# The second layer's products in a new order: 18 up, 15 down, 3 up, 9 down

## The chip, the core and the metric

The kernel runs on one core of a Trainium2 chip. A core has five engines that run side by side, each through its own queue of instructions in the order of the program, and that wait for one another by semaphores: TensorE (matrix products, from SBUF into the banks of PSUM), VectorE and ScalarE (element-wise work, from and to SBUF and PSUM), GpSimd and SyncE (here mostly DMA issue). The metric is the time of one execution on the device in microseconds, as the median of several runs.

## What is computed

```python
X = np.fft.rfft(x, axis=1); Y = X * F; y = np.fft.irfft(Y, n=S, axis=1)   # x: 8 x 3072 x 256
# a mixture of eight experts with one expert per token, 256 -> 1024 -> 256
h = np.maximum(x[mask] @ w1[e], 0.0); out[mask] = gate_w * eom * (h @ w2[e])
# the second layer, on all 24576 tokens, 256 -> 2048 -> 256
h = np.maximum(x @ w_in, 0.0)
return (h * h @ w_out).astype(np.float32)
```

The change is in the last two lines, the second layer.

## The kernel before

The program runs through a spectral stage (two transforms and a filter), a routing and first expert layer, and then the second layer, which is what matters here. It works in tiles of 512 tokens, 48 of them (`NTILE2`), and each tile in eight units (`NU`), each of 256 of the 2048 hidden columns. So `units2` holds 384 units, and the loop at the end of `steps_m` walks over them.

All products are made to nearly single precision from two halves: every operand has a high part and a low part, and one product is three matmuls into the same PSUM bank (high by high, high by low, low by high), each 128 x 128 by 128 x 256.

A unit has an up part and a down part. Up (`up2`) multiplies a 2 x 2 arrangement of blocks (tokens by columns) by seven products in place of eight, Strassen's way in Winograd's form. The sums of weight blocks (`wsh`, `wsl`) and of input blocks (`bh`, `bl`) are made ahead of time. The seven products go into three banks: V gets products 0, 4, 5 and 2 one on top of the other, G gets 3 and 6, P gets 1. Between two products on one bank the partial sum must be read out: ScalarE copies V after product 0 into `s1`, G after product 3 into `p5`, V after product 4 into `u2`, V at the end into `C[:, 2]`. VectorE adds P and `s1` into `C[:, 0]`, V and `p5` into `C[:, 3]`, G and `u2` into `C[:, 1]`. A product that goes onto a bank with a partial sum waits until that sum has been read. V has two banks that alternate from unit to unit (`psH`), G and P have one each (`psX`, `psH2`). In the trace the tile of V and P is called ph, that of G px, and `s1`, `p5`, `u2` are s, p, u.

Then VectorE makes the squared rectified hidden values in one instruction, `q = max(C, 0) * C` (L923), ScalarE casts them to the high part `hh` (L930), and VectorE subtracts to get the low part `hl` (L932); the last two are in `split_h`. Down (`down2`) multiplies `hh` and `hl` by `woh` and `wol`: 24 matmuls (L945) that are summed over the eight units of a tile in two banks (py). In the last unit of a tile each bank is copied out by ScalarE after matmul 11 and 23 (L951) and scattered to the output by DMAs of GpSimd (L954).

All three are Python generators. The order in which the loop resumes them is the order in which each engine gets its instructions; nothing reorders them later. In iteration n the loop interleaves up of unit n, the split of unit n-1 and down of unit n-2, in four parts. Before the change TensorE gets products 0, 3 (six matmuls), down's 0 to 2, products 1, 4, down's 3 to 8, products 6, 5, down's 9 to 17, product 2, down's 18 to 23. One iteration is 21 matmuls of up and 24 of down.

Beside it, the inputs of the next tile are loaded (`load_t`, in unit 2) and split (`split_t`, L865 to L889, one step at the end of each of units 3 to 6).

Of the kernel before, what the change touches and what calls it, by code (L numbers as in the profile page):

```python
# [17 lines left out]
ALU = mybir.AluOpType  # L18
# [84 lines left out]
def spectral_moe_kernel(ctx: ExitStack, tc: tile.TileContext, x, filt_r, filt_i, w_gate, w_og, w1, w2,  # L103
                        w_in, w_out, c_ma, c_mi, c_mb, c_mb2, c_sg, c_cum, out):
    nc = tc.nc
# [608 lines left out]
    def py_tiles(t):  # L714
        return [pl["psY2" if t % 2 and "psY2" in pl else "psY"].tile([128, TT], F32, name=f"py{h}") for h in range(2)]
# [82 lines left out]
    def up(t, f):  # L798
        xh, xl = X[t]
        w = width[t]  # L800
        h1, l1 = (a[:, 0] for a in W[t, f // 2])
        f2 = f % 2
        ps = ph_tile()[:, 0:w]
        n = 0
        for c in range(2):
            for a, b in ((h1, xh), (h1, xl), (l1, xh)):
                nc.tensor.matmul(ps, a[:, c, f2 * 128:(f2 + 1) * 128], b[:, c, 0:w], start=n == 0, stop=n == 5)  # L807
                n += 1
        hh = pl["hp"].tile([128, TT], F32R, name="hh")[:, 0:w]
        hl = pl["hp"].tile([128, TT], F32R, name="hl")[:, 0:w]  # L810
        nc.scalar.activation(hh, ps, AF.Relu)  # L811
        tick[:] = [hh[0:1, 0:1].bitcast(F32)]
        nc.vector.scalar_tensor_tensor(hl, ps, 0.0, hh.bitcast(F32), op0=ALU.max, op1=ALU.subtract)  # L813
        H[t, f] = hh, hl
# [77 lines left out]
    def up2(t, u):  # L892

        bh, bl, _ = X2[t]
        wsh, wsl = w2nd[0:2]

        def prod(ps, a, b, start):
            for n, (x, y) in enumerate(((wsh, bh), (wsh, bl), (wsl, bh))):
                nc.tensor.matmul(ps, x[:, u, a], y[:, b], start=start and n == 0, stop=n == 2, skip_group_check=True)  # L899

        bank = lambda name: pl[name].tile([128, TT], F32, name="px" if name == "psX" else "ph")[:, 0:256]
        V, G, P = bank("psH"), bank("psX"), bank("psH2")
        s1, p5, u2 = (pl["sp"].tile([128, 256], F32, name=n) for n in ("s1", "p5", "u2"))
        C = pl["cp"].tile([128, 4, 256], F32, name="C")
        prod(V, 0, 0, True)
        nc.scalar.copy(s1, V)
        prod(G, 3, 3, True)
        nc.scalar.copy(p5, G)
        yield
        prod(P, 1, 1, True)  # L910
        nc.vector.tensor_tensor(C[:, 0], P, s1, ALU.add)
        prod(V, 4, 4, False)
        nc.scalar.copy(u2, V)
        yield
        prod(G, 6, 2, False)
        prod(V, 5, 5, False)
        nc.vector.tensor_tensor(C[:, 3], V, p5, ALU.add)  # L917
        nc.vector.tensor_tensor(C[:, 1], G, u2, ALU.add)
        yield
        prod(V, 2, 6, False)  # L920
        nc.scalar.copy(C[:, 2], V)  # L921
        q = pl["cp"].tile([128, 4, 256], F32, name="q")
        nc.vector.scalar_tensor_tensor(q, C, 0.0, C, op0=ALU.max, op1=ALU.mult)  # L923
        H2[t, u] = q
        yield

    def split_h(t, u):
        q = H2[t, u]
        hh, hl = (pl["h2p"].tile([128, 4, 256], F32R, name=n) for n in ("hh2", "hl2"))
        nc.scalar.copy(hh, q)  # L930
        yield
        nc.vector.tensor_tensor(hl, q, hh.bitcast(F32), ALU.subtract)  # L932
        H2[t, u] = hh, hl
        yield

    def down2(t, u):

        hh, hl = H2[t, u]
        woh, wol = w2nd[2:4]
        if u == 0:  # L940
            Z[t] = [p.rearrange("p (c d) -> p c d", c=2) for p in py_tiles(t)]
        for m in range(24):
            k, i, c, n = m // 12, m // 6 % 2, m // 3 % 2, m % 3
            x, w = ((hh, woh), (hl, woh), (hh, wol))[n]
            nc.tensor.matmul(Z[t][k][:, c, :], x[:, 2 * i + k, c * 128:(c + 1) * 128], w[:, 2 * u + i, :],  # L945
                             start=u == 0 and m in (0, 12), stop=u == NU - 1 and m in (11, 23), skip_group_check=True)
            if u == NU - 1 and m in (11, 23):
                if k == 0:
                    Z[t].append(pl["oup"].tile([128, 4, D], F32, name="ou"))
                ou = Z[t][2]  # L950
                nc.scalar.copy(ou[:, 2 * k:2 * k + 2, :], Z[t][k])  # L951
                io = X2[t][2]
                for c in range(2 * k, 2 * k + 2):
                    nc.gpsimd.indirect_dma_start(out=outv[4 * t + c], out_offset=bass.IndirectOffsetOnAxis(ap=io[:, c:c + 1], axis=0),  # L954
                                                 in_=ou[:, c, :], in_offset=None)
            if m in (2, 8, 17):
                yield
        del H2[t, u]
        if u == NU - 1:
            del X2[t], Z[t]  # L960
        yield
# [3 lines left out]
    units2 = [(t, u) for t in range(NTILE2) for u in range(NU)]  # L965
# [3 lines left out]
    def step_1(t, f):  # L969

        last = t + 1 == KP
        if f == 5 and t + 2 == KP:
            start_t(KP)
        if f == 1 and t + 1 >= KP:
            for n in (t + 2, t + 3) if last else (t + 3,):
                if n < NMAIN:
                    start_t(n)
        if f == 1 and last:
            gather(KP)
        if f == 3 and t + 2 < NMAIN and t + 2 != KP:  # L980
            gather(t + 2)
        if f % 2 == 1:

            g = NQ * t + f // 2 + 2
            if NQ * KP <= g < NQ * NMAIN:
                split_w(*divmod(g, NQ))
            if NQ * KP <= g + 2 < NQ * NMAIN:
                load_w(*divmod(g + 2, NQ))
        if t + 1 < NMAIN:
            at = (4, 5, 7) if last else (2, 4, 6)  # L990
            if f == at[0]:
                scale_x(t + 1)
            if f == at[0] + 1:
                put_ids(t + 1)
            if f in at[1:]:
                turn_x(t + 1, at.index(f) - 1)
        elif f == 1:
            load_t(0)
            load_t(1)
        if f not in (1, 5) and dec and next(dec[0], 0) == 0:  # L1000
            dec.clear()
            dcs.close()
            pl["bp0"] = ctx.enter_context(tc.tile_pool(name="bp0", bufs=1))
            pl["bp0"].tile([128, 16], F32, name="pad0")
        if t + 1 == NMAIN and f >= 3:
            if f == 3:
                first.append(split_t(0))
            next(first[0], None)

    def extra(t):  # L1010

        start_t(t)
        gather(t)
        for q in range(3):
            load_w(t, q)
        scale_x(t)
        put_ids(t)
        turn_x(t, 0)
        turn_x(t, 1)
        for f in range(NF + 1):  # L1020
            if f < NF:
                if f % 2 == 0:
                    split_w(t, f // 2)
                    if f == 0:
                        load_w(t, 3)
                up(t, f)
            if f:
                down(t, f - 1)

    def rest(t):  # L1030

        if t < NTILE1:
            with tc.If(used[0] > slot[t - KP]):
                extra(t)
                rest(t + 1)
# [3 lines left out]
    def steps_m():  # L1039
        for n in range(len(jobs) + LAG1):  # L1040
            if n < len(jobs):
                t, f = jobs[n]
                up(t, f)
                step_1(t, f)
            if n >= LAG1:
                down(*jobs[n - LAG1])
            yield
        used.append(nc.values_load(usedi[0:1, 0:1], min_val=0, max_val=NTILE_T))
        with tc.If(used[0] > NTILE_T - NX):
            extra(NMAIN)  # L1050
            rest(NMAIN + 1)
        m1.close()
        xgs.close()
        open_m2()
        st = iter(())
        for n in range(len(units2) + 2):
            g = up2(*units2[n]) if n < len(units2) else iter(())
            t, u = units2[min(n, len(units2) - 1)]
            d = down2(*units2[n - 2]) if n >= 2 else iter(())
            for part in range(4):  # L1060
                next(g, None)
                if part == 0 and 0 < n <= len(units2):
                    sh = split_h(*units2[n - 1])
                if part in (1, 2) and n:
                    next(sh, None)
                next(d, None)
            if u == 2 and t + 2 < NTILE2:
                load_t(t + 2)
            if u == 3 and t + 1 < NTILE2:
                st = split_t(t + 1)  # L1070
            next(st, None)
            yield
# [43 lines left out]
    m = steps_m()  # L1116
# [4 lines left out]
    for i, k in enumerate(order):  # L1121
# [3 lines left out]
        n = done["a"]  # L1125
# [62 lines left out]
```

## Time and profile before

| what | us |
|---|---|
| median of 3 runs | 3807.01 (3805.06 to 3810.75) |
| the profiled execution, whole | 3809.94 |
| its span, from first to last instruction | 3808.2 |
| the second layer's matmuls, first to last | 1777.4 to 3797 |

The profile is of one execution. A page sums it up; the rest are answers to questions put to its trace. In the views below a line of the timeline is one instruction: its start from the start of the span, its duration, its engine (PE is TensorE's matmuls, PEld its loads of stationary weights, DVE is VectorE, ACT ScalarE), its line in the program, what it writes and reads, and, in brackets, how long the engine stood idle ahead of it and what it waited for. Matmuls are pipelined, so a matmul's duration is much longer than the distance from its start to the next one's start; the distance is what counts.

### The profile page before, as it was taken

What the parts mean: (1) busy time and instruction counts of PE and PEld (TensorE: products, weight loads), DVE (VectorE), ACT (ScalarE), POOL (GpSimd) and SP (SyncE); (2) the same over time, 40 slices, a digit from 0 to 9 for tenths busy, and PEclk for the clock granted to TensorE, in tenths of its full rate; (3) what the DMA queues carried; (4) which work ended last, traced back from release to release, by engine and by line L of the source; (5) the groups of instructions that cost most, each with busy time, mean ns of one, the idle gap of its engine ahead of it and who ended that gap; (6) DMA issues with size and microseconds to landing.
All of it is one profiled execution on the core that took longest, in us unless ns stands there. A gap on an engine that the chain in (4) does not pass through costs nothing.

```text
span 3808.2 us, 73021 instructions
## 1 busy us (share of the span) xinstructions
PE 3750.1 (98%) x27156; PEld 3501.1 (92%) x27156; DVE 2759.2 (72%) x5024; ACT 1966.4 (52%) x3896; POOL 607.0 (16%) x641
## 2 busy tenths in 40 slices
PE   8999999999999999999999999999999999999998
PEld 7888877888888888888999999999999999999998
DVE  6677685678878875656777777777777777777775
ACT  6466473354545454554555555555555555555554
POOL 3477574000000000000011001000100110011001
PEclk9999999999999999999999999999999999999999
DMA  6333322455555554543000100010000001000100
GB/s 193 101 114 116 105 81 95 149 161 165 174 159 176 165 165 154 158 159 95 24 26 27 29 23 29 23 29 23 29 24 28 24 29 29 23 26 26 29 18 18
DMA packets 259756, 306.63 MB, mean 81 GB/s; under 512 B 74721, under 2 KB 203202, under 8 KB 259394
## 3 DMA queue, kind: packets, MB, share of 16 engines
q1 hardware_dynamic: 239936, 249.75, 21.6%
q0 software_dynamic: 18432, 51.93, 3.8%
q8 instruction: 214, 3.51, 0.4%
q14 instruction: 148, 1.21, 0.1%
q10 hardware_dynamic: 1026, 0.23, 0.0%
HBM read 221.63 MB, written 80.19 MB: 79 GB/s over the span
## 4 chain that ended last, share of the span: by engine, by line
PE 84%; issue 10%; DVE 2%; POOL 1%; DMA 1%; ACT 1%; another core or an unknown queue 0%; DVEq 0%; POOLq 0%; ACTq 0%; SPq 0%
PE py L945 22%; PE ph L899 14%; PE ph L807 14%; PE py L824 14%; PE px L899 6%; PE o L360 3%; PE p L380 3%; PE o L394 2%; PE p L281 2%; PE p L334 1%; PE p L338 1%; PE p L309 1%; POOL out_dram L954 1%; PE px L787 1%; DMA xt<-in_x_dram 0%
## 5 line engine op out<-in xcount | busy, mean ns | idle before, releaser
L945 PE MATMUL py<-woh,hh 128*128 128x256 f32 x3072 | 857.2, 279 | 0.0
L945 PE MATMUL py<-woh,hl 128*128 128x256 f32 x3072 | 852.8, 278 | 0.4 <-DVE hl L932 0.4
L945 PE MATMUL py<-wol,hh 128*128 128x256 f32 x3072 | 852.9, 278 | 0.0
L954 POOL DMA_INDIRECT out_dram<-ou,ix x192 | 213.2, 1110 | 2912.9 <-ACT ou L951 2869.0
L945 PEld LDWEIGHTS py<-woh,hl 128*128 128x128 f32 x3072 | 579.9, 189 | 0.9 <-DVE hl L932 0.8
L945 PEld LDWEIGHTS py<-woh,hh 128*128 128x128 f32 x3072 | 579.9, 189 | 0.0
L945 PEld LDWEIGHTS py<-wol,hh 128*128 128x128 f32 x3072 | 576.3, 188 | 0.0
L899 PE MATMUL ph<-bh,wsh 128*128 128x256 f32 x1920 | 540.9, 282 | 5.9 <-DMA ytd<-yt 4.6
L811 ACT ACTIVATE hh<-ph 128x512 fp32r<-128x512 f32 (+1 forms) x464 | 248.7, 536 | 574.8 <-PE ph L807 548.8
L899 PE MATMUL ph<-bl,wsh 128*128 128x256 f32 x1920 | 537.1, 280 | 0.0
L899 PE MATMUL ph<-bh,wsl 128*128 128x256 f32 x1920 | 536.7, 280 | 0.0
L923 DVE SCALAR_TENSOR_TENSOR q<-C 128x1024 f32<-128x1024 f32 x384 | 470.5, 1225 | 6.4 <-ACT C L921 6.4
L932 DVE TENSOR_TENSOR hl<-q,hh 128x1024 fp32r<-128x1024 f32 x384 | 467.1, 1216 | 1.1 <-ACT hh L930 1.1
L813 DVE SCALAR_TENSOR_TENSOR hl<-ph,hh 128x512 fp32r<-128x512 f32 (+1 forms) x464 | 283.3, 611 | 252.0 <-ACT hh L811 244.2
L917 DVE TENSOR_TENSOR C<-ph,p 128x256 f32<-128x256 f32 x384 | 163.6, 426 | 412.8 <-ACT hh L930 402.5
L921 ACT COPY C<-ph 128x256 f32<-128x256 f32 x384 | 143.4, 373 | 532.4 <-PE ph L899 500.2
L930 ACT CAST hh<-q 128x1024 fp32r<-128x1024 f32 x384 | 402.8, 1049 | 1.3 <-DVE q L923 1.3
L899 PEld LDWEIGHTS ph<-bh,wsh 128*128 128x128 f32 x1920 | 362.3, 189 | 7.1 <-issue 4.7
L899 PEld LDWEIGHTS ph<-bl,wsh 128*128 128x128 f32 x1920 | 360.9, 188 | 0.0
L899 PEld LDWEIGHTS ph<-bh,wsl 128*128 128x128 f32 x1920 | 360.8, 188 | 0.0
L824 PE MATMUL py<-hh,wh 128*128 128x512 f32 (+1 forms) x928 | 336.6, 369 | 0.0
L807 PE MATMUL ph<-xh,wh 128*128 128x512 f32 (+1 forms) x928 | 335.2, 361 | 0.0
(265 smaller groups left out, 8045.4 us busy)
## 6 DMA issues: line engine op xcount, KB each, us to landing
r<-in_moe_w_dram SPq DMA_DIRECT2D x440, 256.0 KB
xt<-in_x_dram SPq DMA_DIRECT2D x48, 512.0 KB
r<-ytd SPq DMA_DIRECT2D x48, 512.0 KB
xg<-srt SPq DMA_DIRECT2D x41, 544.0 KB
ytd<-yt SPq DMA_DIRECT2D x41, 512.0 KB
xg<-srt SPq DMA_DIRECT2D x17, 272.0 KB
ytd<-yt SPq DMA_DIRECT2D x17, 256.0 KB
raw<-in_moe_w_in_dram SPq DMA_DIRECT2D x16, 256.0 KB
```

Of the source, the lines that this page charges most:

```text
L807: nc.tensor.matmul(ps, a[:, c, f2 * 128:(f2 + 1) * 128], b[:, c, 0:w], start=n == 0, stop=n == 5)
L811: nc.scalar.activation(hh, ps, AF.Relu)
L813: nc.vector.scalar_tensor_tensor(hl, ps, 0.0, hh.bitcast(F32), op0=ALU.max, op1=ALU.subtract)
L824: nc.tensor.matmul(Y[t][h], a[:, f % 2, h * 128:(h + 1) * 128], b, start=f == 0 and i == 0, stop=f == NF - 1 and i == 2, skip_group_check= ...
L899: nc.tensor.matmul(ps, x[:, u, a], y[:, b], start=start and n == 0, stop=n == 2, skip_group_check=True)
L917: nc.vector.tensor_tensor(C[:, 3], V, p5, ALU.add)
L921: nc.scalar.copy(C[:, 2], V)
L923: nc.vector.scalar_tensor_tensor(q, C, 0.0, C, op0=ALU.max, op1=ALU.mult)
L930: nc.scalar.copy(hh, q)
L932: nc.vector.tensor_tensor(hl, q, hh.bitcast(F32), ALU.subtract)
L945: nc.tensor.matmul(Z[t][k][:, c, :], x[:, 2 * i + k, c * 128:(c + 1) * 128], w[:, 2 * u + i, :], start=u == 0 and m in (0, 12), stop=u == ...
L954: nc.gpsimd.indirect_dma_start(out=outv[4 * t + c], out_offset=bass.IndirectOffsetOnAxis(ap=io[:, c:c + 1], axis=0), in_=ou[:, c, :], in_o ...
```

## The change

It moves the points at which `up2` and `down2` give control back, and the loop's calls. Up of a unit now reaches into the next iteration: the loop keeps the generator of the unit before in `old` and resumes it three times, once for product 2 (behind product 0 of the new unit), once for ScalarE's copy into `C[:, 2]` (behind the copy into `p5`), once for VectorE's square (behind the sum into `C[:, 0]`). TensorE's order in iteration n becomes: product 0 of unit n, product 2 of unit n-1, products 3, 1, 4, 6 of unit n, down's 0 to 14 of unit n-2, product 5 of unit n, down's 15 to 23. ScalarE's order: `s1`, `p5`, `C[:, 2]` of unit n-1, `u2`, `hh` of unit n-1. VectorE's: `C[:, 0]`, the square of unit n-1, `C[:, 1]`, `C[:, 3]`, `hl` of unit n-1.

```diff
         prod(V, 0, 0, True)
         nc.scalar.copy(s1, V)
+        yield
         prod(G, 3, 3, True)
         nc.scalar.copy(p5, G)
         yield
         prod(P, 1, 1, True)
         nc.vector.tensor_tensor(C[:, 0], P, s1, ALU.add)
+        yield
         prod(V, 4, 4, False)
         nc.scalar.copy(u2, V)
-        yield
         prod(G, 6, 2, False)
+        nc.vector.tensor_tensor(C[:, 1], G, u2, ALU.add)
+        yield
         prod(V, 5, 5, False)
         nc.vector.tensor_tensor(C[:, 3], V, p5, ALU.add)
-        nc.vector.tensor_tensor(C[:, 1], G, u2, ALU.add)
         yield
         prod(V, 2, 6, False)
+        yield
         nc.scalar.copy(C[:, 2], V)
+        yield
         q = pl["cp"].tile([128, 4, 256], F32, name="q")
         nc.vector.scalar_tensor_tensor(q, C, 0.0, C, op0=ALU.max, op1=ALU.mult)
         H2[t, u] = q
...
-            if m in (2, 8, 17):
+            if m in (5, 14):
                 yield
...
         st = iter(())
+        none = iter(())
+        old = none
         for n in range(len(units2) + 2):
-            g = up2(*units2[n]) if n < len(units2) else iter(())
+            g = up2(*units2[n]) if n < len(units2) else none
             t, u = units2[min(n, len(units2) - 1)]
-            d = down2(*units2[n - 2]) if n >= 2 else iter(())
-            for part in range(4):
-                next(g, None)
-                if part == 0 and 0 < n <= len(units2):
-                    sh = split_h(*units2[n - 1])
-                if part in (1, 2) and n:
-                    next(sh, None)
-                next(d, None)
+            d = down2(*units2[n - 2]) if n >= 2 else none
+            next(g, None)
+            next(old, None)
+            next(g, None)
+            next(old, None)
+            next(g, None)
+            next(old, None)
+            sh = split_h(*units2[n - 1]) if 0 < n <= len(units2) else none
+            next(g, None)
+            next(sh, None)
+            next(d, None)
+            next(d, None)
+            next(g, None)
+            next(sh, None)
+            next(d, None)
+            old = g
             if u == 2 and t + 2 < NTILE2:
```

## Rows read from the trace of the kernel before

**Rows 1.** The page: the span, and each engine's busy time.

```profile
span 3808.2 us, 73021 instructions
PE 3750.1 (98%) x27156; PEld 3501.1 (92%) x27156; DVE 2759.2 (72%) x5024; ACT 1966.4 (52%) x3896; POOL 607.0 (16%) x641
```

**Rows 2.** Table by stretch: length, busy time per engine, granted clock, DMA share, GB/s.

```profile
1800.00:3790.00 1990.00, 1990.00 (x17065) 1989.74 (x17064) 1464.93 (x2270) 1033.33 (x2175) 209.35 (x188) 1.00 0.09 26
```

**Rows 3.** Timeline, TensorE: one unit's blocks by first matmul, and twenty units on.

```profile
2605.18 0.28 PE L899 MATMUL ph<-bh,wsh 128*128 128x256 f32 x1
...
2606.25 0.28 PE L899 MATMUL ph<-bh,wsh 128*128 128x256 f32 x1
...
2606.60 0.28 PE L899 MATMUL ph<-bh,wsh 128*128 128x256 f32 x1
...
2607.62 0.28 PE L899 MATMUL px<-bh,wsh 128*128 128x256 f32 x1
...
2608.34 0.28 PE L945 MATMUL py<-woh,hh 128*128 128x256 f32 x1
...
2609.40 0.28 PE L899 MATMUL ph<-bh,wsh 128*128 128x256 f32 x1
...
2610.43 0.28 PE L899 MATMUL ph<-bh,wsh 128*128 128x256 f32 x1
...
2710.14 0.28 PE L899 MATMUL ph<-bh,wsh 128*128 128x256 f32 x1
```

**Rows 4.** Timeline: a weight load, a product's last matmul, and copies of idle ScalarE.

```profile
2606.49 0.28 PE L899 MATMUL ph<-bh,wsl 128*128 128x256 f32 x1
2606.49 0.19 PEld L899 LDWEIGHTS ph<-bh,wsh 128*128 128x128 f32 x1
...
2606.83 0.28 PE L899 MATMUL ph<-bh,wsl 128*128 128x256 f32 x1
...
2607.20 0.37 ACT L913 COPY u<-ph 128x256 f32<-128x256 f32 x1 [0.57 <-PE ph L899]
...
2611.04 0.37 ACT L906 COPY s<-ph 128x256 f32<-128x256 f32 x1 [0.66 <-PE ph L899]
```

**Rows 5.** Timeline, the layer's first units: loads that wait, and matmuls behind them.

```profile
1782.90 0.37 ACT L906 COPY s<-ph 128x256 f32<-128x256 f32 x1
...
1783.32 0.19 PEld L899 LDWEIGHTS ph<-bh,wsh 128*128 128x128 f32 x1
...
1783.54 0.28 PE L899 MATMUL ph<-bl,wsh 128*128 128x256 f32 x1
...
1784.02 0.28 PE L899 MATMUL px<-bh,wsl 128*128 128x256 f32 x1
...
1785.61 0.19 PEld L899 LDWEIGHTS ph<-bh,wsh 128*128 128x128 f32 x1 [0.79 <-DVE C L917]
...
1785.83 0.28 PE L899 MATMUL ph<-bl,wsh 128*128 128x256 f32 x1
...
1786.07 0.28 PE L899 MATMUL ph<-bh,wsh 128*128 128x256 f32 x1
...
1786.41 0.28 PE L899 MATMUL px<-bh,wsh 128*128 128x256 f32 x1
```

**Rows 6.** Groups of instructions, 1800 to 3790 us: busy us, mean ns, idle before.

```profile
L930 ACT CAST hh<-q 128x1024 fp32r<-128x1024 f32 x380 | 398.6, 1049 | 0.0
...
L923 DVE SCALAR_TENSOR_TENSOR q<-C 128x1024 f32<-128x1024 f32 x379 | 464.4, 1225 | 5.6 <-ACT C L921 5.6
L932 DVE TENSOR_TENSOR hl<-q,hh 128x1024 fp32r<-128x1024 f32 x379 | 461.0, 1216 | 0.0
...
L885 DVE TENSOR_TENSOR tc<-r,tc 128x256 f32<-128x256 f32 x94 | 39.6, 421 | 1.6
```

**Rows 7.** Timeline, the layer's end: the last product 2, and the last load that waits.

```profile
3790.15 0.28 PE L899 MATMUL ph<-bh,wsh 128*128 128x256 f32 x1
...
3794.78 0.19 PEld L945 LDWEIGHTS py<-woh,hl 128*128 128x128 f32 x1 [0.59 <-DVE hl L932]
```

More of the change, by code (lines that the diff above doesn't have):

```diff
@@ L911, in up2 @@
         nc.vector.tensor_tensor(C[:, 0], P, s1, ALU.add)
+        yield
         prod(V, 4, 4, False)
         nc.scalar.copy(u2, V)
+        prod(G, 6, 2, False)
+        nc.vector.tensor_tensor(C[:, 1], G, u2, ALU.add)
         yield
-        prod(G, 6, 2, False)
         prod(V, 5, 5, False)
         nc.vector.tensor_tensor(C[:, 3], V, p5, ALU.add)
-        nc.vector.tensor_tensor(C[:, 1], G, u2, ALU.add)
         yield
         prod(V, 2, 6, False)
+        yield
         nc.scalar.copy(C[:, 2], V)
+        yield
         q = pl["cp"].tile([128, 4, 256], F32, name="q")
```

## Prediction

> **What bounds the kernel now.** I read the page first: its span is 3808.2 us and TensorE is busy for 98% of it [rows 1]. A busy TensorE need not be one at its peak, so the second view is the table by stretch: from 1800 to 3790 us, which is the second layer, TensorE has 1990.00 us of work in 1990.00 us, 17065 matmuls, with a granted clock of 1.00, the 2.4 GHz level [rows 2]. That is 0.1166 us for each matmul, 5.248 us for a unit of 45. The timeline says the same: twenty units from 2605.18 to 2710.14 take 104.96 us [rows 3]. VectorE is busy for 1464.93 us of the stretch and ScalarE for 1033.33, so both have room, and nothing but the matmuls' own spacing, or a new wait of TensorE, moves the end.
>
> The third view is one unit by its matmuls [rows 3]. The reader should see that the spacing is not one number. Nine matmuls from 2606.60 to 2607.62 come every 0.1133 us; nine from 2608.34 to 2609.40 every 0.1178 us. I call these paces quick and slow. The clock is the same in both. The pace changes where a stretch of down products gives way to up products: at 2605.18 to slow, at 2606.25 to quick, at 2607.62 to slow, at 2609.40 to quick, at 2610.43 to slow again, four changes in a unit. Where up gives way to down (2608.34, for one) the pace is kept. All quick, a unit would be 45 x 0.1133 = 5.10 us. The first slow block costs 2606.25 - 2605.18 - 9 x 0.1133 = 0.05 us, the second 2609.40 - 2607.62 - 15 x 0.1133 = 0.08, and each quick block 0.01 to get going (1.37 against 12 x 0.1133, 1.03 against 9 x 0.1133). Together 0.15, which is the 5.248 measured.
>
> **The change: what stays.** Per unit there are the same 45 matmuls and the same ten instructions of ScalarE and VectorE. No DMA is added; the two output copies and four output DMAs of a tile's last unit keep their places behind down's matmuls 11 and 23. What changes is the order. Call the products by their operand's place: V0, G3, P1, V4, G6, V5, V2. The loop now gives TensorE V0, V2 of the unit before, G3, P1, V4, G6 (18 matmuls), fifteen of down, V5 (three), nine of down. ScalarE gets s1, p5, the copy of C[:,2] of the unit before, u2, the cast hh; VectorE gets C[:,0], the square, C[:,1], C[:,3], then hl.
>
> **The change: the new wait.** G6 adds onto the bank that G3 filled, and p5 must have read that bank first. Before, fifteen matmuls lay between the two. Now only P1 and V4 do, six matmuls. The way from G3's last matmul to the load of G6's weights goes by three rows. From the start of a product's last matmul to the start of an idle ScalarE's copy: 2607.20 - 2606.83 = 0.37 us [rows 4]. The copy: 0.37 us [rows 4]. From a copy's end to the load that it lets go: s1 ended at 1782.90 + 0.37 = 1783.27, the load came at 1783.32, so 0.05 [rows 5]. Sum 0.79 us. ScalarE is idle when G3 ends: s1 starts 2611.04 - 2610.43 = 0.61 us into a unit [rows 3, 4] and takes 0.37, while p5 can start only 8 x 0.1133 + 0.37 = 1.28 us into it. The load is due when the matmul before it starts, as at 2606.49 in [rows 4], so 6 x 0.1133 = 0.68 us after G3's last: it is 0.11 us late in every unit. After such a wait nothing is caught up: a held load went at 1785.61, the second matmul behind it at 1785.83, twice a quick step, and two more took 0.24 us to 1786.07 [rows 5], against 0.227 quick, so 0.01 more. Price: 0.12 us per unit. Bounds: nothing, if the wait held the matmul and not its load (below), and 0.13, with the rows' roundings against it.
>
> The Trainium skill, "TensorE: Matmul & The Clock Gate", section "Architectural detail: the array is 16× 32×32, not 1× 128×128", says that TensorE's queue can pull weight loads ahead of matmuls in flight. By that rule the load would not be late, and the wait would cost nothing. The trace does not bear it out for a load that has to wait: the load at 1785.61 stands behind the wait for C [rows 5].
>
> **The change: the pace.** Two changes from down to up are left of four, at V0 and at V5. The trace before has no block of 18 or 15, so the pace of each is bounded by the two that it has. I take it that the pace still turns over at each such change. Which half is slow then hangs on the pace after the new wait. Rows for that lie far apart: after the full stop at 1785.61 the three matmuls from 1786.07 to 1786.41 were quick, while after the load that was only 0.05 us late at 1783.32 four matmuls took 1784.02 - 1783.54 = 0.48 us, slow [rows 5]. At 0.11 us the load starts when its matmul was due, as in a full stop, so I take quick. G6 and fifteen of down are then quick, V5 and nine of down slow, and V0 turns to quick again. A slow block of twelve lies between the block of nine (0.05) and that of fifteen (0.08): 0.065, and 0.01 to get going. Unit: 5.10 + 0.12 + 0.075 = 5.295 us, 0.047 more than 5.248; times 384 units, +18 us.
>
> **The change: other waits.** V4 waits for s1, nine matmuls after V0, as before. V5 waits for u2, now 18 matmuls after V4 where it was nine; V2 for C[:,3], twelve after V5. G3 waits for C[:,1] and P1 for C[:,0] of the unit before, both most of a unit old. The longest chain is the copy of C[:,2], then the square at 1.225 us, the cast hh at 1.049, and hl at 1.216 [rows 6]: the copy ends 2.0 us into the unit, the square by 3.3, hh by 4.4; C[:,1] fits behind the square, C[:,3] at 4.4 behind V5, and hl ends about 0.8 us into the next unit. Down's first use of it there is 18 x 0.1133 + 0.12 = 2.2 us into that unit, 1.4 us of room. Behind hl stands the next tile's preparation in four units of eight: at most four subtractions of 0.421 us [rows 6] or one of hl's size, which pushes C[:,0] and the square back by about 0.6 us; hh then ends by 5.0, and hl still has 1.2 us of room. On ScalarE a late cast or output copy can push s1 by 0.1 us where V4 gives it 0.2 us. I cost all this at nothing. If the room were not there, each late unit would pay by what hl is late; only four units of eight could be.
>
> At the end V2 of the last unit starts the chain to its last down product: 3790.15 to 3794.78, 4.63 us, of which TensorE waits about 0.6 at the end [rows 7]. Six of the down matmuls that lay behind V2 now lie ahead of it, 6 x 0.1178 = 0.7 us more of waiting: +0.7 us. The start of the layer, where no down products exist, is worth 1 us either way, an estimate from its few waits of that size in [rows 5].
>
> **The sum.** The profiled execution took 3809.94 us, 1.7 us over its span and 2.9 over the median of 3807.01. +18 + 0.7 gives 3828.6 on its scale, and 3826 on the median's, which I predict.
>
> **Rivals.** First, the pace after the wait is slow: the 0.48 us row speaks for it, the full stop against. If V0 to V4, G6 and the fifteen are all slow, 33 matmuls cost about 33 x 0.005 = 0.165 (0.08 / 15 a matmul), the wait 0.79 - 6 x 0.1178 = 0.08 and starts 0.02: 5.365 us, +45 us, 3852. If only G6 and the fifteen are slow, 18 x 0.005 + 0.12 + 0.01 = 0.22: 5.32, +28 us, 3835. Second, the other side: the pace does not turn over at V5 or V0 but stays quick, since what turns it may be the number of down products ahead (three and nine led to quick, six to slow; fifteen and nine would both be odd multiples of three). Then the wait alone stands: 5.10 + 0.12 = 5.22 to 5.225 with the small starts, -8 to -10 us, 3798. The sign turns where the wait falls under 0.15 us less what the slow blocks still cost. Third, the wait holds only the matmul: that one is due 7 x 0.1133 = 0.79 us after G3's last, just when the copy is seen, so the stall is nil, the unit 5.10 + 0.075 = 5.175, -28 us, 3780; with all quick 3751. The rule of the Trainium skill told above, in "TensorE: Matmul & The Clock Gate", would give this time; the held load in [rows 5] speaks against it.
>
> **How the numbers follow.** Forecast 0.42; slow after the wait 0.27 (3835 to 3852); all quick with the wait 0.14; no stall 0.14; the rest, 0.03, near no change. Measurement can tell about 0.2%, 7.6 us. Slower: 0.42 + 0.27 = 0.69. Faster: 0.14 for no stall less a small part that ends near no change, 0.12, and half of the second rival, 0.07: 0.19. Same: 0.12. The range leaves out the no-stall rival and the far end of the first: 3797 to 3848.
>
> **What would show it.** In the changed kernel's timeline the load of px after V4 should start 0.05 us behind the end of p's copy and 0.11 us late in each unit, with ScalarE's p named as what it waited for, some 40 us in all; the table by stretch should show idle TensorE; nine of down behind V5 should run at 0.1178. If loads of px come on time, the chain is mis-sized and the third rival holds; if idle time is there but both down stretches run at 0.1133, the second; if fifteen run at 0.1178, the first.

## The result and the profile after

| | before | after |
|---|---|---|
| median, side by side | 3808.88 us (3805.06 to 3811.67, 4 runs) | 3838.95 us (3838.15 to 3840.96, 4 runs) |
| profiled execution, whole | 3809.94 us | 3840.96 us |
| second layer's matmuls, from first to last | 2019.9 us | 2057.0 us |
| steady unit of 45 matmuls | 5.248 us | 5.340 us |

The ratio is 1.0082 (95% interval 1.007 to 1.0095): slower by 30 us. The forecast was slower by 19, to 3826, in a range of 3797 to 3848.

The page of the changed kernel, span and busy time, which answers [rows 1], and the table by stretch, which answers [rows 2]:

```profile
span 3839.3 us, 72546 instructions
...
PE 3785.0 (99%) x27156; PEld 3530.3 (92%) x27156; DVE 2758.3 (72%) x5024; ACT 1992.8 (52%) x3896; POOL 619.1 (16%) x641
...
1800.00:3790.00 1990.00, 1989.44 (x16757) 1982.48 (x16756) 1439.48 (x2231) 1041.95 (x2141) 217.70 (x185) 1.00 0.09 25
```

Same work, same clock, TensorE as busy as before, and 16757 matmuls in the 1990 us where there were 17065. So hardly any of the loss stands as idle time; it has to be read from the matmuls' distances. The timeline of TensorE, one unit by the first matmul of each block, and the first matmul of the same block twenty units on, answers [rows 3]:

```profile
2609.95 0.28 PE L949 MATMUL py<-woh,hh 128*128 128x256 f32 x1
...
2611.72 0.28 PE L899 MATMUL ph<-bh,wsh 128*128 128x256 f32 x1
...
2612.07 0.28 PE L949 MATMUL py<-woh,hh 128*128 128x256 f32 x1
...
2613.09 0.28 PE L899 MATMUL ph<-bh,wsh 128*128 128x256 f32 x1
...
2614.74 0.28 PE L899 MATMUL ph<-bh,wsl 128*128 128x256 f32 x1
2614.86 0.36 PE L899 MATMUL px<-bh,wsh 128*128 128x256 f32 x1
2615.06 0.28 PE L899 MATMUL px<-bl,wsh 128*128 128x256 f32 x1
...
2615.29 0.28 PE L949 MATMUL py<-woh,hh 128*128 128x256 f32 x1
...
2716.76 0.28 PE L949 MATMUL py<-woh,hh 128*128 128x256 f32 x1
```

Twenty units take 106.81 us, 5.340 each. Fifteen of down: 2611.72 - 2609.95 = 1.77 us, 0.118 a matmul, slow. Nine of down behind V5: 1.02 us, 0.1133, quick. V0 to V4 and G6's first: fifteen steps in 1.77 us, slow. Between the first and the second matmul of G6 lie 0.20 us where a slow step is 0.118: that is the new wait, 0.08 us. The pace turns over at V0 and at V5, and 33 of 45 matmuls are slow.

The wait by its chain (weight loads of TensorE, ScalarE's copy), which answers [rows 4]:

```profile
2614.04 0.28 PE L899 MATMUL px<-bh,wsl 128*128 128x256 f32 x1
...
2614.41 0.37 ACT L909 COPY p<-px 128x256 f32<-128x256 f32 x1 [0.33 <-PE px L899]
...
2614.63 0.19 PEld L899 LDWEIGHTS ph<-bh,wsl 128*128 128x128 f32 x1
2614.83 0.19 PEld L899 LDWEIGHTS px<-bh,wsh 128*128 128x128 f32 x1
```

G3's last matmul to p's start 0.37, the copy 0.37, its end at 2614.78 to the load at 2614.83 0.05: the 0.79 of the forecast to the hundredth. The load was due with V4's last matmul, at 2614.74, and stood 0.09 later. But the view of waits from 1800 to 3790 us (what waited, for whom: us in total, times, longest) hardly shows it:

```profile
PEld px L899 <- ACT p L909: 1.8, 6, 0.3
```

A load takes 0.19 us and the next one starts 0.12 after it, so a load that is 0.08 late leaves no gap between the bars; only the distance of the starts shows it.

The layer's end, the last product 2, the last load that waits, and the last matmul, answers [rows 7]:

```profile
3821.12 0.28 PE L899 MATMUL ph<-bh,wsh 128*128 128x256 f32 x1
...
3825.75 0.19 PEld L949 LDWEIGHTS py<-woh,hl 128*128 128x128 f32 x1 [0.95 <-DVE hl L936]
...
3828.45 0.28 PE L949 MATMUL py<-wol,hh 128*128 128x256 f32 x1
```

Product 2 to the last waiting load is again 4.63 us. TensorE's waits there are 0.95 and, for the cast half of the unit before, 0.36 at 3821.91: 1.31 where it was 0.59.

The layer grew by 37.0 us, of which the units are 383 x (5.3447 - 5.2490) = 36.7 by their means (the few units of 5.63 included). In this execution it began at 1771.5 us, 5.95 earlier than in the profile of before. In the other runs below, whose code ahead of the layer is the same, it began between 1760.1 and 1778.1: that is the run, not the change. 37.0 - 5.95 is the 31.1 by which the spans differ.

### The profile page after: what moved, and what is told of

Read it like the earlier page. It is cut to its first block, busy times and chain, and to the rows that moved or that the text cites. A ratio compares the mean times of both kernels' runs of the same rounds, so it can differ in the third digit from the quotient of the medians.

```text
span 3839.3 us, 72546 instructions
## 1 busy us (share of the span) xinstructions
PE 3785.0 (99%) x27156; PEld 3530.3 (92%) x27156; DVE 2758.3 (72%) x5024; ACT 1992.8 (52%) x3896; POOL 619.1 (16%) x641
## 4 chain that ended last, share of the span: by engine, by line
PE 38%; issue 14%; POOL 2%; ACT 0%; DVE 0%; POOLq 0%; ACTq 0%
PE py L949 20%; PE ph L899 13%; PE px L899 6%; POOL out_dram L958 2%; ACT p L909 0%; DVE q L927 0%; POOLq L1197 0%; DVE C L920 0%; ACT ou L955 0%; DVE C L917 0%; ACT C L924 0%; POOLq L958 0%; DVE C L912 0%; ACT hh L934 0%; ACTq L955 0%
## 5 line engine op out<-in xcount | busy, mean ns | idle before, releaser
L958 POOL DMA_INDIRECT out_dram<-ou,ix x192 | 225.0, 1172 | 2938.1 <-ACT ou L955 1742.1
L906 ACT COPY s<-ph 128x256 f32<-128x256 f32 x384 | 143.3, 373 | 436.5 <-PE ph L899 360.2
```

## The experiments

**What follows the wait.** The forecast took the pace behind G6 to be quick, and it was slow. First the same wait, made longer: products 1 and 3 change places, so that three matmuls and not six lie between G3 and G6.

```diff
-        prod(G, 3, 3, True)
-        nc.scalar.copy(p5, G)
-        yield
         prod(P, 1, 1, True)
         nc.vector.tensor_tensor(C[:, 0], P, s1, ALU.add)
         yield
+        prod(G, 3, 3, True)
+        nc.scalar.copy(p5, G)
+        yield
...
             next(g, None)
-            next(old, None)
             next(g, None)
             next(old, None)
+            next(old, None)
```

> The changed kernel with the products 3 and 1 changed about, so that only V4 (three matmuls) lies between G3 and G6, and the wait for the copy p5 is longer: 0.79 us less 3 x 0.115 = 0.44 us per unit, a full stop, where the changed kernel had 0.078. It asks what the pace behind a wait hangs on. (A) By its length, as the prediction took it: behind a full stop G6 and the fifteen of down are quick, V5 and the nine of down slow, V0 to V4 quick; unit 5.10 + 0.45 + 0.075 = 5.62 us, program about 3946 us. (B) Behind any wait the pace is slow: V0 to V4 and the fifteen slow, unit 5.30 - 0.03 + 0.44 + 0.01 = 5.72, program about 3985; if only G6 and the fifteen are slow, 5.66 and 3961. (C) The pace goes through the wait unchanged: either of the two, mixed from tile to tile.

Measured: 3940.09 us in one run (before 3797.1 on that chip), 370 of 381 units, first of fifteen to first of fifteen, at 5.62 us. The view of waits from 1800 to 3900 us, then one unit of TensorE's timeline as above:

```profile
PEld px L899 <- ACT p L912: 141.2, 374, 0.7
...
2645.86 0.28 PE L949 MATMUL py<-woh,hh 128*128 128x256 f32 x1
...
2647.56 0.28 PE L899 MATMUL ph<-bh,wsh 128*128 128x256 f32 x1
...
2647.92 0.28 PE L949 MATMUL py<-woh,hh 128*128 128x256 f32 x1
...
2648.98 0.28 PE L899 MATMUL ph<-bh,wsh 128*128 128x256 f32 x1
...
2651.03 0.38 PE L899 MATMUL px<-bh,wsh 128*128 128x256 f32 x1 [0.18 <-ACT p L912]
...
2651.48 0.28 PE L949 MATMUL py<-woh,hh 128*128 128x256 f32 x1
```

Fifteen of down in 1.70 us are quick, nine in 1.06 are slow: (A), to the length of the unit. The stop of 0.44 us leaves the quick pace, as the forecast took it. But here V0 to V4 were quick in every unit, so the run does not show what this stop leaves when it is met from the slow side. Whether the forecast's rule holds at 0.11 us is the next question. The changed kernel with one more change from down to up in one unit of sixteen, so that the next unit meets its wait from the quick side:

```diff
-            if m in (5, 14):
+            if m in (5, 14) or m == 2 and (8 * t + u + 2) % 16 == 12:
...
+            if n % 16 == 12:
+                next(d, None)
             next(g, None)
             next(sh, None)
```

> The changed kernel, but in one unit of sixteen three matmuls of down stand between P1 and V4, which takes the wait of G6 away in that unit and turns the pace over, so that the next unit comes to its wait from the quick pace. It asks whether the state that the prediction forecast (0.11 us of wait, the fifteen quick, unit 5.295) can last. (A) It can't: a wait of 0.11 us met out of the quick pace leaves the slow pace, so one or two units near 5.29 and then 5.340 again; layer 2 and program as the changed kernel, 3838 us less up to 2. (B) It can: stretches of sixteen units of 5.292 next to stretches of 5.340, program 3838 - 384 / 2 x 0.048 = 3829.

Measured: layer 2054.6 us, 2.3 less than the changed kernel; program 3841.2 us in one run, before 3806.52. Timeline of TensorE from the extra turn (V4 at 2691.16) to the next unit's fifteen:

```profile
2691.16 0.28 PE L899 MATMUL ph<-bh,wsh 128*128 128x256 f32 x1
...
2691.86 0.28 PE L949 MATMUL py<-woh,hh 128*128 128x256 f32 x1
...
2693.22 0.28 PE L899 MATMUL ph<-bh,wsh 128*128 128x256 f32 x1
...
2694.64 0.28 PE L899 MATMUL ph<-bh,wsh 128*128 128x256 f32 x1
...
2696.35 0.38 PE L899 MATMUL px<-bh,wsh 128*128 128x256 f32 x1
2696.57 0.28 PE L899 MATMUL px<-bl,wsh 128*128 128x256 f32 x1
...
2696.80 0.28 PE L949 MATMUL py<-woh,hh 128*128 128x256 f32 x1
...
2698.57 0.28 PE L899 MATMUL ph<-bh,wsh 128*128 128x256 f32 x1
```

Twelve of down from 2691.86 are quick (1.36 us), V0 to G6's first from 2694.64 are quick (1.71 for fifteen), the wait is 0.22 - 0.113 = 0.11 us as forecast, and the fifteen behind it are slow (1.77). So it went behind each of the 24 extra turns, within one or two units. (A): the forecast unit exists (5.292 us from one first of fifteen to the next, 5.295 forecast), but it lasts once. In all 47 units in which a wait of 0.11 us was met from the quick side and V4 had not been held, it left the slow pace.

From the slow side the record is not so clean. In 282 units a wait of 0.08 us left the slow pace, but in 20 it left the quick one, as here (V0, G6's first, first of fifteen, V5):

```profile
1883.41 0.28 PE L899 MATMUL ph<-bh,wsh 128*128 128x256 f32 x1
...
1885.18 0.36 PE L899 MATMUL px<-bh,wsh 128*128 128x256 f32 x1
...
1885.60 0.28 PE L949 MATMUL py<-woh,hh 128*128 128x256 f32 x1
...
1887.30 0.28 PE L899 MATMUL ph<-bh,wsh 128*128 128x256 f32 x1
```

Fifteen steps in 1.77 us ahead of the wait, fifteen of down in 1.70 behind it. The changed kernel itself has one such unit, against 371 that stayed slow. The next unit meets its wait from the quick side and is slow again, so these escapes cost or gain little. What sets them apart was not found.

**The wait alone, and the turning over.** The changed kernel (run e1_g3_ahead) with G3 ahead of the old unit's product 2: nine matmuls between G3 and G6, no wait.

```diff
             next(g, None)
-            next(old, None)
             next(g, None)
             next(old, None)
+            next(old, None)
             next(g, None)
```

> The changed kernel with one step moved: G3 with the copy p5 comes right behind V0, ahead of product 2 of the unit before, so nine matmuls in place of six lie between G3 and G6. Both theories: the load of px for G6 is due 9 x 0.1178 = 1.06 us after G3's last matmul and is let go after 0.79, so TensorE's wait for p, 0.078 us a unit in the changed kernel, goes: at least 30 us less than its 3839. Theory A (the pace turns over at each change from down to up, whatever happens between, and the start of the layer decides which half is slow): the unit is 5.27 us, 3813, if 18 up and fifteen down are slow, or 5.17 us, 3775, if five's three and nine down are. Theory B (it is the short wait behind V4 that makes the long block slow): the long block is quick, 5.17 us, 3775, for certain.

Measured: 3791.49 us (5 runs) against 3806.93 (9 runs), ratio 0.9959 (0.9945 to 0.9974): faster than both kernels. Its layer is 2000.9 us. One unit of either kind, as they start (fifteen of down, V5, the next unit's fifteen):

```profile
2595.38 0.28 PE L949 MATMUL py<-woh,hh 128*128 128x256 f32 x1
...
2597.08 0.28 PE L899 MATMUL ph<-bh,wsh 128*128 128x256 f32 x1
...
2600.55 0.28 PE L949 MATMUL py<-woh,hh 128*128 128x256 f32 x1
...
1970.37 0.28 PE L949 MATMUL py<-woh,hh 128*128 128x256 f32 x1
...
1972.14 0.28 PE L899 MATMUL ph<-bh,wsh 128*128 128x256 f32 x1
...
1975.64 0.28 PE L949 MATMUL py<-woh,hh 128*128 128x256 f32 x1
```

304 units are of the first kind (fifteen quick in 1.70; 5.173 us), 36 of the second (slow in 1.77; 5.267). Against the changed kernel's 5.340 the second kind differs by the wait alone: 0.073 us. The first kind differs from the second by the pace alone: 0.094. Most of the other units are 34 in which ScalarE's copy into `s1` came about 0.4 us late and held V4, 0.2 us of unit each; some of those stalls threw the pace over. What delayed that copy was not found; in the next run it happened once. Neither theory came out whole: most units have the long block quick, as (B) says, but 36 are slow in stretches of up to fifteen with no wait behind V4, as (A) allows. The time is 16 us over the 3775 of both. The slow units and the stalls are 10 of that, and some 6 are the early start of the run whose 3839 the texts counted from.

That the pace turns over at each change from down to up, and is not a property of a block, is tested by an extra change in one unit of sixteen of this kernel, with the edit of the run before.

> The order of e1_g3_ahead, but in one unit of sixteen (iterations 12, 28, 44, ...) three matmuls of down are put between P1 and V4, so that this unit alone has three changes from down to up products where the others have two. No work and no wait is added. (A) The pace turns over at each change from down to up: at each such unit the two paces change places, and stay changed until the next such unit or the next stall: units of 5.173 us (long block quick) in stretches of sixteen next to stretches of 5.267 (long block slow), about half of each; program some 0.09 x 384 / 2 less what e1_g3_ahead already had of slow units, about +14 us on 3791: 3805. (B) The pace belongs to the place in the unit or to what stalled last: the extra cut changes at most its own unit, units stay at 5.173 mostly, program 3791 to 3793.

Measured: 3783.99 us beside 3797.1 for before. The layer is 2010.0 us, 9.1 more than without the turns. Eight units at 2612.30 to 2653.68, ahead of the extra turn at V4 (2658.52), and eight from 2690.48, behind it:

```profile
2612.30 0.28 PE L949 MATMUL py<-woh,hh 128*128 128x256 f32 x1
...
2653.68 0.28 PE L949 MATMUL py<-woh,hh 128*128 128x256 f32 x1
...
2658.52 0.28 PE L899 MATMUL ph<-bh,wsh 128*128 128x256 f32 x1
...
2690.48 0.28 PE L949 MATMUL py<-woh,hh 128*128 128x256 f32 x1
...
2692.25 0.28 PE L899 MATMUL ph<-bh,wsh 128*128 128x256 f32 x1
...
2732.61 0.28 PE L949 MATMUL py<-woh,hh 128*128 128x256 f32 x1
```

41.38 / 8 = 5.173 us, then 42.13 / 8 = 5.266, fifteen of down in 1.77. From the first extra turn on, the whole layer goes by turns: the unit with the extra turn, then fifteen of the one kind, the next such unit, then fifteen of the other, without an exception. (A). The edit of one unit sets the time of the next fifteen.

**The place of the operands.** Is the order all that sets the pace? The pad ahead of the layer's pools is changed: with 16 columns the tiles of `bh`, `bl` (all but the first tile's), `hh` and `hl` lie 64 bytes below a multiple of 1024, with 8, 32 and 64 columns 32, 128 and 256 bytes below; the weight tiles lie at multiples of 1024. Nothing else differs from the changed kernel, from before, and from the order of e1_g3_ahead (twice).

```diff
-        right(ctx, "pad2", 1).tile([128, 16], F32, name="pad2")
+        right(ctx, "pad2", 1).tile([128, 32], F32, name="pad2")
```

> The changed kernel with its order as it is, but the pad ahead of the second layer's tiles is 128 bytes in place of 64, so that bh, bl, hh and hl all lie 64 bytes lower; wsh, wsl, woh and wol stay. If the pace is a matter of order alone (theory A and theory B), nothing changes: 3839 and the two paces 0.1133 and 0.1178. If it is a matter of where the operands lie against each other (theory C), the spacing of the matmuls changes: another pace than those two, or the long block quick. The wait for p stays at 0.08 to 0.11 us.

> The kernel before with the pad ahead of the second layer's tiles at 128 bytes in place of 64, nothing else. Order alone (A, B): 3809, the four turns of the pace in a unit as before. Place (C): the slow blocks' spacing changes, with 0.15 us a unit, 57 us in all, to be lost or as much again to be paid.

> The order of e1_g3_ahead with the pad ahead of the second layer's operands at 8 columns in place of 16, so that the input's and the hidden values' tiles lie 32 bytes higher against the weights. No work, wait or order is changed. (A) The pace is set by the order of products alone: two states, 5.173 and 5.267 us, program 3791 us. (B) It is set by where the two operands of a matmul and of the weight load beside it lie in SBUF as well, as the runs with a pad of 32 columns showed: the unit leaves these two values; with spacings like those of that pad, 0.1183 on the mean and no wait, 5.32 us and 3849.

> The order of e1_g3_ahead with the pad at 64 columns in place of 16: the tiles lie 192 bytes lower against the weights, at a multiple of 256 bytes from them. (A) The pace is set by the order of products alone: 5.173 and 5.267 us, program 3791 us. (B) It is set by the place: as with a pad of 32 columns 5.32 us and 3849; as in the first expert layer, where all operands begin at multiples of 1024 bytes and a matmul takes 0.120 us, 5.40 us and 3878.

| pad | order | program (before beside it) | unit | matmuls' distance |
|---|---|---|---|---|
| 32 | changed | 3871.52 (3806.93) | 5.406 | 0.112 to 0.124, 0.118 on the mean; wait 0.08 |
| 32 | before | 3843.39 (3806.93) | 5.340 | 0.112 to 0.128, 0.1187 on the mean |
| 8 | e1_g3_ahead | 3816.74 (3797.1) | 5.284 and 5.316, by turns | 0.113 to 0.125 |
| 64 | e1_g3_ahead | 3854.18 (3797.1) | 5.400 | 0.120 throughout |

With 64 columns, from one unit's first of down to the one twenty units on:

```profile
2610.68 0.28 PE L949 MATMUL py<-woh,hh 128*128 128x256 f32 x1
...
2718.68 0.28 PE L949 MATMUL py<-woh,hh 128*128 128x256 f32 x1
```

108.00 / 20 / 45 = 0.120. Each row is one run, but the differences are several times the spread of the kernels that ran more often. The place counts in all four: of the places tried, only the one with 16 columns has two lasting paces that turn over. 16 columns in place of 32 are worth 36 us to the kernel before, more than the change. With 32 columns the changed order is slower too, by 28 us and 0.066 us a unit, a little less than its wait: there the wait accounts for the whole loss, and no pace comes on top.

**A version that beats both.** If the unit must have a slow block, let it be short: the order of e1_g3_ahead with down cut as 21 and 3 (run e2_short_second), so that V5 and three are the block between the turns.

```diff
-            if m in (5, 14):
+            if m in (5, 20):
```

> As the run with G3 ahead, and down is split after 21 matmuls in place of fifteen: blocks of 18 up with 21 down, and three up with three down. Theory A: six matmuls are of one pace and 39 of the other. If the long block is quick, a unit costs 5.10 + 6 x 0.005 + 0.02 = 5.15 us, 3766; if it is slow, 5.10 + 39 x 0.005 + 0.02 = 5.31, 3830. Theory B: the long block is quick, 3766. A third theory, that a fixed share of a unit is slow however it is cut: 5.2 to 5.25 us, about the kernel before.

Measured: 3822.36 us, ratio 1.0042 (1.0028 to 1.0056), slower. The two kinds are 5.147 (107 units) and 5.293 (204), but in up to two units of eight V4 or V2 is held up, the stalls throw the pace over, and most units end up with the long block slow. Then with the next tile's preparation ahead of product 5 (run e9_short_early), and the same with one extra turn in iteration 12:

```diff
+            if u == 3 and t + 1 < NTILE2:
+                st = split_t(t + 1)
+            next(st, None)
             next(g, None)
...
-            if u == 3 and t + 1 < NTILE2:
-                st = split_t(t + 1)
-            next(st, None)
```

> The order of e2_short_second (18 up with G3 ahead, 21 of down, 3 up, 3 of down), with the next tile's preparation moved ahead of product 5 in each iteration, so that ScalarE's cast of the prepared blocks comes before, not behind, the point at which it has to read V0. It asks whether the stall of V4 in two units of eight was that cast. If it was: no units of 5.38 to 5.45 us, and the pace no longer thrown over in each tile: units of 5.147 us (long block quick) or 5.293 (long block slow), whichever the layer's start leaves, for hundreds of units; program 3770 to 3775 by the one, 3825 by the other. If not: the same stalls, 3822.

> As e9_short_early, and in iteration 12 alone three matmuls of down stand between P1 and V4, one more change from down to up. By the theory that each such change turns the pace over, this kernel is in the other state from iteration 12 on: where the one has units of 5.147 us, the other has 5.293, and the two programs differ by up to 370 x 0.146 = 54 us, as long as no stall comes in between. If the cut of one unit out of 384 doesn't matter beyond that unit, the two agree within 1 us.

Measured: 3807.1 us, ratio 1.0 (0.9991 to 1.001), and 3808.84, ratio 1.0005 (0.9995 to 1.0015): no change. V4's stall is gone, so it was the preparation's place, and in the trace of the run before, the cast ends just where the late copy into `s1` starts (1890.5 us). But V2 now waits for C[:,3] 76 times between 1800 and 3790 us, 0.25 to 0.45 us of lost time each, and these stalls set the pace anew: 63 and 39 slow units. The pair says nothing on the single turn, since no state lasted long enough.

These stalls show that a stop's length alone does not set the pace behind it. Of the 61 that were met from the quick side (0.26 to 0.45 us), 45 left the quick pace and 16 the slow one; of the 15 met from the slow side (0.25 us), 10 left quick and 5 slow. Two of 0.37 us, both met from the quick side, each from V2's second matmul to the first of down:

```profile
1876.05 0.28 PE L899 MATMUL ph<-bl,wsh 128*128 128x256 f32 x1
...
1877.30 0.28 PE L949 MATMUL py<-woh,hh 128*128 128x256 f32 x1
...
3179.36 0.28 PE L899 MATMUL ph<-bl,wsh 128*128 128x256 f32 x1
...
3180.66 0.28 PE L949 MATMUL py<-woh,hh 128*128 128x256 f32 x1
```

Eleven steps in 1.25 us, quick, and in 1.30, slow; the units behind them are 5.147 and 5.293. What else the pace hangs on is open.

At last the preparation's first step goes back to the end of unit 3:

```diff
-            if u == 3 and t + 1 < NTILE2:
-                st = split_t(t + 1)
-            next(st, None)
+            if u != 3:
+                next(st, None)
...
             if u == 2 and t + 2 < NTILE2:
                 load_t(t + 2)
+            if u == 3 and t + 1 < NTILE2:
+                st = split_t(t + 1)
+                next(st)
```

> As e9_short_early, but the first step of the next tile's preparation (three copies of ScalarE, three subtractions of VectorE, in unit 3) goes back behind VectorE's hl, and only the later steps stay ahead of product 5. In e9_short_early product 2 was held 0.3 to 0.45 us behind the sum C[:,3] in 45 of 48 tiles' fourth iteration. If the three subtractions ahead of C[:,3] do that, these 45 stalls of some 0.37 us go, 17 us, and 3807 becomes about 3790, less what fewer slow units give back (63 units of 5.293 in that run, 0.146 each, 9 us at most): 3781 to 3790. If the stall is of another cause, 3807.

Measured: 3772.11 us (4 runs) against 3793.55 (7 runs), ratio 0.9946 (0.993 to 0.9963): the fastest of all, 21 us under before. The view of waits from 1800 to 3740 us, and VectorE in a unit 4:

```profile
PEld ph L899 <- DVE C L920: 11.6, 46, 0.3
...
1865.83 0.41 DVE L885 TENSOR_TENSOR tc<-r 128x256 f32<-128x256 f32 x1
...
1867.29 0.42 DVE L920 TENSOR_TENSOR C<-ph,p 128x256 f32<-128x256 f32 x1
```

No unit of 5.293 is left, and each stall of this run left the quick pace. One stall per tile stays, moved to the next unit: four subtractions from 1865.83 on stand ahead of C[:,3] (1867.29), and such a unit takes 5.473, not 5.147, some 15 us in all. So the preparation's first step ahead of C[:,3] was the cause of the stalls in each tile's fourth unit; its three subtractions stood there behind ScalarE's three copies, which they wait for. The layer is 24.6 us shorter than in e9_short_early. Counted by unit over 5.147, the 47 units with that stall cost 17.2 there, 29 with a stall of V2 one unit earlier 13.8, and 63 slow units 9.2; the 47 new ones cost 15.4 here. What had caused the 29 is open. The changed order as such was not at fault; its wait and the pace behind the wait were.

## Why the prediction was right, and where its steps were not

The sign and the range were right, and the branch was wrong: the step that failed is "so I take quick", in the part on the pace. That the time fell into the range is in part luck. The rival whose mechanism came true, with 33 slow matmuls, was priced at 3852, outside the range; it came out cheaper than its own sum, and the layer of the profiled execution began 6 us early.

- **The unit without the wait.** The third rival gives 5.175 us for long block quick, V5 and nine slow. Measured without the wait: 5.173. The turning over at V0 and V5, by the rows of before alone, held in every unit without a stall; behind some stalls (7 units of e1_g3_ahead, 8 of e9_short_early) the pace stayed slow at V5.
- **The second rival** (number of down products decides, all quick) fell: nine, an odd multiple of three, led to slow at V0 in the changed kernel.
- **The wait.** Its chain of 0.79 us held to the hundredth, and so did 0.11 us from the quick side (0.22 - 0.113 behind the extra turns). Since V0 to V4 ran slow, it was 0.08, as the first rival has it; in the unit 0.073.
- **The pace behind it.** Forecast quick, measured slow. [rows 5] held both answers: a full stop left quick, a load 0.05 us late left slow. I took the row of the full stop, because at 0.11 us the load starts when its matmul was due. In the runs 0.11 us met from the quick side left slow 47 times of 47, and the 0.44 us at the same place left quick. But length is not all: stalls of 0.25 to 0.45 us at V2 left either pace. So no border of length was found, and why this wait leaves slow is open.
- **The sum.** 5.173 + 0.094 (pace) + 0.073 (wait) = 5.340; forecast 5.175 + 0.12 = 5.295. The pace was missed by +0.094, the wait over-estimated by 0.047: net 0.045 x 384 = 17 us more than +18.7, 36 for the layer, which measured +37. The layer's earlier start in that execution took 6 back: 31 on the span, 30 by the medians. The kernel with the extra turns, which pays the same wait in nearly every unit, was 35 over before. The first rival, with 0.27, had the right mechanism: all 33 slow, and 5.365. Its 0.02 for getting going is hardly there.
- **Other waits** cost nothing in the steady unit, as forecast, but for some six units of 5.63 in which V4 was late, 2 us in all. The tail was +0.7, as forecast: 1.31 - 0.59.
- **The third rival**, a wait for the matmul alone, fell: the load itself stood 0.08 us late in every unit. The reorder rule of the Trainium skill ("TensorE: Matmul & The Clock Gate", section "Architectural detail: the array is 16× 32×32, not 1× 128×128") gave nothing back here: 0.073 of the 0.08 us stands in the unit.
- **What would show it.** Fifteen at 0.118 told at once that the first rival held. My 40 us of idle TensorE was a bad sign to look for: a load held for less than its own overlap leaves no gap.

## What to carry to other kernels

Where a stream of matmuls is the bound, measure the distance of their starts, block by block, before counting work: the same 45 matmuls took 5.15 to 5.41 us here, by their order, a wait of 0.08 us and their operands' place, with hardly any idle time to see. A short wait can come with a slow pace behind it that costs more than its length (0.094 against 0.073 us here), so look for a reordering that takes it away (here one call moved turned +0.8% into -0.4%). And a result that hangs on such a state has to be tried at another operand offset before the order is given the credit.

## What the runs showed of the hardware

- With the 2.4 GHz level granted throughout (1.00), a 128x128 load with a 128x256 matmul on these halves (fp32r) came every 0.1133, 0.118 or 0.120 us. With a pad of 16 columns the quick or the slow state can last for hundreds of units. It is turned over by each change from down to up products, in all units without a stall, and in none of these by the other change.
- What a wait leaves: 0.44 us at G6, met from the quick side, quick in every unit; 0.11 us there, met from the quick side, slow in all 47; 0.08 us, met from the slow side, slow in 282 and quick in 20 of one run. Stalls of 0.25 to 0.45 us at V2 left either. What decides it is open.
- Moving the moving and the stationary operand by 32 to 192 bytes against each other changed all of this, the unit by up to 4.4% (5.173 to 5.400, with 16 and 64 columns). The Trainium skill, "SBUF — State Buffer", section "Who interferes with whom", gives TensorE two read ports, one for the moving operand and one for the weight load, as independent. These runs don't show which part of the way the place acts on; they do show that it acts.
